# Two of the sixteen attention features of each head copied by DMA into the zero rows of the last block of gated features, for the output projection

## The chip, the cores and the metric

The kernel runs on one core of a Trainium2 chip. Its time is in device microseconds (us), the median of several executions. The core has a matrix engine (TensorE, PE in the profile; its weight loads are PEld), a vector engine (VectorE, DVE), an activation engine (ScalarE, ACT), a general engine (GpSimd, POOL) and a queue engine (SyncE, SP) from which this kernel issues every transfer. Transfers themselves run on sixteen DMA engines.

## What is computed

A normalised sequence x of 2048 tokens with 512 features goes through two branches, and both results are added to x. Branch A is attention with 32 heads of 16 features, where a token looks at 8 positions (itself and every second one before it), followed by a projection with `wo`. Branch B is a gated network: 688 features `z1`, gated by 688 others mixed over all tokens, and projected with `w_out`.

```python
xn = _layernorm(x, axis=-1)
return x + _A_ref(xn, A_wqkv, A_wo) + _B_ref(xn, B_w_in, B_w_sp, B_b_sp, B_w_out)
# _A_ref: S = 2048, D = 512, H = 32, Dh = 16, W = 8, dil = 2
o = jnp.einsum('bhsw,bhswd->bhsd', attn, vg)
return o.transpose(0, 2, 1, 3).reshape(B, S, D) @ wo
# _B_ref: Fh = 688
z = _gelu(jnp.einsum('bsd,df->bsf', x, w_in))
z1 = z[..., :Fh].copy()
z2 = _layernorm(z[..., Fh:], axis=-1)
g = jnp.einsum('ts,bsf->btf', w_sp, z2) + b_sp[None, :, None]
return jnp.einsum('bsf,fd->bsd', z1 * g, w_out)
```

## The kernel before

Tokens stand in 16 tiles of 128. The first part of the kernel (to about 75 us) normalises x, computes the second half of branch B's features, and queries, keys and values. The middle part runs from 75 to 172 us, one iteration a token tile `j`: `mix(j)` (L458) multiplies the tile's rows of `w_sp` with all of `z2`, `z1_tile(j)` (L470) computes the tile's `z1`, and `gate_out(j)` (L482) multiplies the two on DVE (L484) and issues from SP a transposing DMA (L485) that writes the gated tile into `uT`. `uT` holds features on partitions and tokens along its free axis, in 6 blocks (`MCH`) of 128 features. Only 688 of these 768 are real: the last block has 48 rows of features (`FTAIL`) and 80 rows of zeros, which come from columns of `z1` that POOL sets to zero (L478). The weights `wout` have the same 6 blocks; POOL sets the whole last block to zero (L511), and DMAs then fill the real rows (L562, L563).

Meanwhile DVE works through `av_ops` (L513): weighting of values by the attention, a tree of adds, and at L530 a write of `op`. `op` holds the attention output with one group of 256 tokens on each 32 partitions (one partition a head), the 16 features of a head (`DH`) and the two halves of the sequence (`hb`, 256 columns each) along its free axis. So partition 32k + h, feature d, column 256 hb + t is head h at token 1024 hb + 256 k + t. `vector_work(us)` (L538) lets DVE take the next pieces of that work between other instructions of its queue. The weights `wo_r` are laid out alike, a copy for each group of 32 partitions, by four DMAs (L566).

The last part, from 172 us, is the output projection (L574 to L598). It runs as two pairs; a pair is one half of the sequence. For each pair PE first runs, for both of its column blocks `jj`, for each `d` of 16 and each `k` of 4, a product of 32 rows (L583); the four `k` use four row groups of PE (`tile_position`) and four accumulators. Then for each of the 8 accumulators it adds the 6 blocks of `uT` times `wout` (L591), 128 rows each. When an accumulator is complete, DVE adds x to it (L595) and SP stores it (L596). The accumulators of a column block are one PSUM pool of four banks, so the second pair's products for a block start when the first pair's additions of that block are done. After each column block of the first pair, SP also loads the x rows for the second pair (`load_xr`, L548 and L550). The stores use four buffers `ot`.

The schedule is written by hand: each engine takes its instructions in the order of the text. SP issues transfers in that order, and before it issues one it waits for the transfer eight places earlier in its order, because eight completion semaphores are used in rotation.

Of the kernel before, what the change touches and what calls it, by code (L numbers as in the profile page):

```python
# [7 lines left out]
BF16 = mybir.dt.bfloat16  # L8
# [5 lines left out]
P = 128  # L14
S = 2048
D = 512
NT = S // P
C = D // P
H = 32
DH = 16  # L20
W = 8
DIL = 2
HALO = 16
NB = 2
SB = S // NB
NG = 4
TG = SB // NG
# [3 lines left out]
MCH = 6  # L31
# [13 lines left out]
def kernel(  # L45
# [18 lines left out]
    G = nc.gpsimd  # L64
    PE = nc.tensor
    SP = nc.sync
# [39 lines left out]
    for c in range(C):  # L106
# [3 lines left out]
                        base=15 - 128 * c, pattern=[[16, 32]], channel_multiplier=-1)  # L110
    mask = const.tile([32, W, HALO], F32, name="mask")
    G.memset(mask[:], 0.0)
    G.affine_select(out=mask[:], in_=mask[:], compare_op=ALU.is_ge, fill=NEG,
                    base=-DIL * (W - 1), pattern=[[DIL, W], [1, HALO]], channel_multiplier=0)
    b_col = const.tile([P, NT], F32, name="b_col")
# [14 lines left out]
    z2 = base.tile([P, NT, FH], BF16, name="z2")  # L130
    a_sb = base.tile([P, W, NB * TG], BF16, name="a_sb")
    vp = base.tile([P, DH, NB, HALO + TG], BF16, name="vp")
    w_z1 = base.tile([P, C, FH], BF16, name="w_z1")
# [127 lines left out]

    wv_v = wv[:].rearrange("p k (h d) -> p k d h", d=DH)
    xnT_g = xnT[:].rearrange("p c (b k t) -> p c b k t", b=NB, k=NG)
# [12 lines left out]
    def shifted(ap):  # L276

        return bass.AP(ap.tensor, ap.offset, [ap.ap[0], [DIL, 2]] + list(ap.ap[1:]))

    lg = [lgp.tile([P, W, TG], BF16, name="lg") for _ in range(NB)]  # L280
    prs = {}

    def products(hb, p):
        pr = prp.tile([P, 2, C, SB], BF16, name="pr")
        off = HALO - DIL * (W - 1 - 2 * p)
        V.tensor_tensor(pr[:], qk[hb][:, 0, :, HALO:HALO + SB].unsqueeze(1).broadcast_to([P, 2, C, SB]),  # L286
# [3 lines left out]
    def reduce_heads(hb, p):  # L290
        pr = prs.pop((hb, p))
        pl = ps_aux.tile([P, 2, TG], F32, name="pl", tag="aux")
        for c in range(C):
            for k in range(NG):
                PE.matmul(pl[32 * k:32 * k + 32, :, :], rsel[:, c, :], pr[:, :, c, k * TG:(k + 1) * TG],  # L295
                          start=(c == 0), stop=(c == C - 1), tile_position=(0, 32 * k))
        A.activation(lg[hb][:, 2 * p:2 * p + 2, :], pl[:], ACT.Copy, scale=float(DH) ** -0.5)

    def softmax_top(hb):
# [6 lines left out]
        V.tensor_tensor(m4[:, 0, :], m4[:, 0, :], m4[:, 1, :], ALU.max)  # L306
        V.tensor_tensor(l[:], l[:], m4[:, 0, :].unsqueeze(1).broadcast_to([P, W, TG]), ALU.subtract)

# [146 lines left out]
    uT = late.tile([P, MCH, S], BF16, name="uT")  # L455
    gate = {}

    def mix(j):  # L458
        pg = bank_pair("pg", j > 3)
        for k in range(NT):  # L460
            for hh in range(2):
                PE.matmul(pg[:, hh, 0:FHALF], wsps[j][:, k, :], z2[:, k, hh * FHALF:(hh + 1) * FHALF],  # L462
                          start=(k == 0), stop=(k == NT - 1))
        gs = gsp.tile([P, 2, FHALF], BF16, name="gs")
        A.activation(gs[:], pg[:, :, 0:FHALF], ACT.Identity, bias=b_col[:, j:j + 1])  # L465
        if j + 5 < NT:
            load_wsp(j + 5)
        return gs

    def z1_tile(j, gs):  # L470
        pz = bank_pair("pz1", j > 3)
        for hh in range(2):
            for kc in range(C):
                PE.matmul(pz[:, hh, 0:FHALF], xnT[:, kc, j * P:(j + 1) * P],  # L474
                          w_z1[:, kc, hh * FHALF:(hh + 1) * FHALF],
                          start=(kc == 0), stop=(kc == C - 1))
        z1 = z1p.tile([P, FPAD], BF16, name="z1")
        G.memset(z1[:, FH:FPAD], 0.0)  # L478
        A.activation(z1[:, 0:FH].rearrange("p (a b) -> p a b", a=2), pz[:, :, 0:FHALF], ACT.Gelu_apprx_tanh)  # L479
        gate[j] = (gs, z1)  # L480

    def gate_out(j):  # L482
        gs, z1 = gate.pop(j)
        V.tensor_tensor(z1[:, 0:FH], gs[:].rearrange("p a b -> p (a b)"), z1[:, 0:FH], ALU.mult)  # L484
        SP.dma_start_transpose(uT[:, :, j * P:(j + 1) * P], z1[:])  # L485
# [17 lines left out]
    late2 = ctx.enter_context(tc.tile_pool(name="late2", bufs=1, reuse_waits="tile", **right))  # L503
# [2 lines left out]
    smp = ctx.enter_context(tc.tile_pool(name="smp", bufs=1, reuse_waits="tile", **right))  # L506
    otp = ctx.enter_context(tc.tile_pool(name="otp", bufs=4, reuse_waits="tile", **right))
    op = late2.tile([P, DH, NB * TG], BF16, name="op")
    wo_r = late2.tile([P, DH, D], BF16, name="wo_r")
    wout = late2.tile([P, MCH, D], BF16, name="wout")  # L510
    G.memset(wout[:, MCH - 1, :], 0.0)  # L511

    def av_ops():  # L513
        for hb in range(NB):
            for q in range(2):
                osl = slice(hb * TG + q * P, hb * TG + (q + 1) * P)
                pws = []
                for p in range(4):
                    off = HALO - DIL * (W - 1 - 2 * p) + q * P
                    pw = pwp.tile([P, 2, DH, P], BF16, name="pw")  # L520
                    V.tensor_tensor(pw[:], shifted(vp[:, :, hb, off:off + P]),  # L521
# [16 lines left out]
    def vector_work(us):  # L538
        while us > 0:
            t = next(work, None)  # L540
            if t is None:
                return
            us -= t
# [4 lines left out]
    def load_xr(jj):  # L548
        xr = xrp.tile([P, NG, D], BF16, name="xr")
        SP.dma_start(xr[:], x_g[jj // 2, jj % 2])  # L550
        xrs.append(xr)

    vector_work(2.0)
    for j in range(3, NT):
        z1_tile(j, mix(j))
        if j == 3:
            pair_b.close()
            ps_o = [ctx.enter_context(tc.tile_pool(name="ps_o0", bufs=4, space=PSUM, reuse_waits="tile"))]
        vector_work(4.6)
        gate_out(j - 1)  # L560
        if j == 5:
            SP.dma_start(wout[:, 0:MCH - 1, :], B_w_out[0:(MCH - 1) * P, :].rearrange("(m p) n -> p m n", p=P))  # L562
            SP.dma_start(wout[0:FTAIL, MCH - 1, :], B_w_out[(MCH - 1) * P:FH, :])  # L563
        if 6 <= j < 10:
            k = j - 6
            SP.dma_start(wo_r[32 * k:32 * k + 32, :, :], A_wo.rearrange("(h d) n -> h d n", d=DH))  # L566
        if 11 <= j < 13:
            load_xr(j - 11)
    gate_out(NT - 1)
    pair_a.close()  # L570

# [2 lines left out]
    for pair in range(2):  # L574
        if pair:
            vector_work(1e9)
        pos = {}
        for jj in (2 * pair, 2 * pair + 1):
            for k in range(NG):
                pos[jj, k] = ps_o[jj % 2].tile([P, D], F32, name="po")  # L580
            for d in range(DH):
                for k in range(NG):
                    PE.matmul(pos[jj, k][:], op[32 * k:32 * k + 32, d, jj * P:(jj + 1) * P],  # L583
                              wo_r[32 * k:32 * k + 32, d, :],
                              start=(d == 0), stop=False, tile_position=(32 * k, 0))
        for jj in (2 * pair, 2 * pair + 1):
            hb, q = jj // 2, jj % 2
            for k in range(NG):
                i = 8 * hb + 2 * k + q
                for m in range(MCH):  # L590
                    PE.matmul(pos[jj, k][:], uT[:, m, i * P:(i + 1) * P], wout[:, m, :],  # L591
                              start=False, stop=(m == MCH - 1))
                vector_work(2.0)
                ot = otp.tile([P, D], BF16, name="ot")
                V.tensor_tensor(ot[:], pos[jj, k][:], xrs[jj][:, k, :], ALU.add)  # L595
                SP.dma_start(out2[i * P:(i + 1) * P, :], ot[:])  # L596
            if jj + 2 < 4:
                load_xr(jj + 2)  # L598
# [30 lines left out]
```

## Time and profile before

| What | us |
|---|---|
| median of 3 runs (212.54 to 212.78) | 212.76 |
| time of the profiled execution | 212.73 |
| its span in the profile | 210.8 |
| PE busy, of the span | 204.5 (97%) |
| DVE busy | 166.7 (79%) |
| ACT busy | 93.1 (44%) |
| 256 matmuls of 32 rows, L583 | 14.2 |
| 96 matmuls of 128 rows, L591 | 21.1 |
| 16 additions on DVE, L595 | 10.8 |

The span is the stretch that the profiler sees, from the first to the last event of the program; the time is longer by what lies around it. Busy times are sums over an engine's instructions. Matmuls overlap in PE's pipeline: the mean duration of one, 374 ns at L583, is its latency and not its share of PE's time, for which the busy time of the group or the chain of work is to be read. The granted clock of PE is full in every slice of the page.

### The profile page before, as it was taken

What the parts mean: (1) busy time and instruction counts of PE and PEld (TensorE: products, weight loads), DVE (VectorE), ACT (ScalarE), POOL (GpSimd) and SP (SyncE); (2) the same over time, 40 slices, a digit from 0 to 9 for tenths busy, and PEclk for the clock granted to TensorE, in tenths of its full rate; (3) what the DMA queues carried; (4) which work ended last, traced back from release to release, by engine and by line L of the source; (5) the groups of instructions that cost most, each with busy time, mean ns of one, the idle gap of its engine ahead of it and who ended that gap; (6) DMA issues with size and microseconds to landing.
All of it is one profiled execution on the core that took longest, in us unless ns stands there. A gap on an engine that the chain in (4) does not pass through costs nothing.

```text
span 210.8 us, 4012 instructions
## 1 busy us (share of the span) xinstructions
PE 204.5 (97%) x1677; PEld 119.2 (57%) x1677; DVE 166.7 (79%) x198; ACT 93.1 (44%) x144; POOL 6.0 (3%) x34
## 2 busy tenths in 40 slices
PE   7899999999999999999999999999999999999992
PEld 5445545445556665566666666666666654444440
DVE  4689977978169699999999999999999943771252
ACT  2457987766788997328522222222222220000000
POOL 5000000000000000000000000000000000000000
PEclk9999999999999999999999999999999999999999
DMA  6992444999000004533975899999763121048022
GB/s 174 316 331 65 83 82 96 153 278 194 3 0 3 3 0 37 124 63 76 170 172 113 218 212 176 199 192 183 157 167 92 37 40 37 25 115 262 28 100 75
DMA packets 67953, 25.56 MB, mean 121 GB/s; under 512 B 56880, under 2 KB 67808, under 8 KB 67808
## 3 DMA queue, kind: packets, MB, share of 16 engines
q1 hardware_dynamic: 67936, 25.31, 55.9%
q8 instruction: 13, 0.21, 0.4%
q14 instruction: 4, 0.03, 0.0%
HBM read 9.98 MB, written 2.10 MB: 57 GB/s over the span
## 4 chain that ended last, share of the span: by engine, by line
PE 94%; DMA 3%; DVE 1%; SPq 1%; ACT 0%; issue 0%
PE pg L462 36%; PE pq L257 13%; PE po L591 10%; PE pz L474 9%; PE pzb L225 9%; PE po L583 7%; PE pv L270 7%; PE pl L295 4%; DMA w_z<-in_B_w_in_dram 3%; DVE xnT L216 0%; DVE ot L595 0%; ACT xnT L214 0%; SPq L170 0%; PE pt L212 0%; SPq L166 0%
## 5 line engine op out<-in xcount | busy, mean ns | idle before, releaser
L462 PE MATMUL pg<-z,wspT 128*128 128x344 bf16 x512 | 77.3, 309 | 0.0
L462 PEld LDWEIGHTS <-wspT 128*128 128x128 bf16 x512 | 49.9, 98 | 25.2 <-issue 0.8
L286 DVE TENSOR_TENSOR pr<-qk 128x8192 bf16<-128x8192 bf16 x8 | 35.1, 4420 | 6.5 <-PE pl L295 6.5
L465 ACT ACTIVATE gs<-pg,b_col 128x688 bf16<-128x688 f32 x16 | 13.4, 835 | 54.0 <-PE pg L462 54.0
L521 DVE TENSOR_TENSOR pw<-vp,a_sb 128x4096 bf16<-128x4096 bf16 x16 | 36.1, 2284 | 0.0
L257 PE MATMUL pq<-xnT,wqk 128*128 128x512 bf16 x128 | 29.1, 379 | 0.4 <-DVE xnT L216 0.4
L595 DVE TENSOR_TENSOR ot<-po,xr 128x512 bf16<-128x512 f32 x16 | 10.8, 688 | 18.2 <-PE po L591 17.3
L225 PE MATMUL pzb<-w_z,xnT 128*128 128x344 bf16 x128 | 20.8, 310 | 0.9 <-DMA w_z<-in_B_w_in_dram 0.7
L474 PE MATMUL pz<-w_z,xnT 128*128 128x344 bf16 x128 | 21.3, 309 | 0.0
L591 PE MATMUL po<-wout,uT 128*128 128x512 bf16 x96 | 21.1, 379 | 0.0
L257 PEld LDWEIGHTS <-wqk 128*128 128x128 bf16 x128 | 12.3, 98 | 15.0 <-issue 1.4
L260 ACT CAST qk<-pq 128x1024 bf16<-128x1024 f32 x16 | 16.2, 1012 | 8.4 <-PE pq L257 8.2
L526 DVE TENSOR_TENSOR pw<-pw 128x4096 bf16<-128x4096 bf16 x8 | 18.3, 2288 | 0.1
L225 PEld LDWEIGHTS <-xnT 128*128 128x128 bf16 x128 | 12.1, 98 | 9.1 <-issue 1.7
L474 PEld LDWEIGHTS <-xnT 128*128 128x128 bf16 x128 | 12.4, 98 | 6.8 <-issue 0.8
L591 PEld LDWEIGHTS <-uT 128*128 128x128 bf16 x96 | 9.2, 98 | 11.7 <-issue 0.8
L270 PE MATMUL pv<-xnT,wv 128*32 128x512 bf16 x256 | 14.9, 380 | 0.0
L479 ACT ACTIVATE z<-pz 128x688 bf16<-128x688 f32 x16 | 11.9, 744 | 5.6 <-PE pz L474 4.8
L583 PE MATMUL po<-wo_r,op 32*128 32x512 bf16 x256 | 14.2, 374 | 0.0
L235 ACT ACTIVATE junk<-z 128x688 bf16<-128x688 bf16 x16 | 12.5, 780 | 0.1
L231 ACT ACTIVATE z<-pzb 128x688 bf16<-128x688 f32 x16 | 11.8, 739 | 0.6 <-PE pzb L225 0.6
L270 PEld LDWEIGHTS <-wv 128*32 128x32 bf16 x256 | 9.4, 138 | 4.7 <-issue 0.3
(73 smaller groups left out, 142.3 us busy)
## 6 DMA issues: line engine op xcount, KB each, us to landing
wo_r<-in_A_wo_dram SPq DMA_DIRECT2D x4, 512.0 KB, 5.4
xr<-in_A_x_dram SPq DMA_DIRECT2D x4, 512.0 KB, 4.1
out_dram<-ot SPq DMA_DIRECT2D x16, 128.0 KB, 1.7
xq<-in_A_x_dram SPq DMA_DIRECT2D x3, 512.0 KB, 6.7
wqk<-in_A_wqkv_dram SPq DMA_DIRECT2D x4, 256.0 KB, 6.2
w_z<-in_B_w_in_dram SPq DMA_DIRECT2D x2, 344.0 KB, 4.7
w_z<-in_B_w_in_dram SPq DMA_DIRECT2D x1, 688.0 KB, 6.9
wout<-in_B_w_out_dram SPq DMA_DIRECT2D x1, 640.0 KB, 5.4
```

Source lines behind the costliest of these rows:

```text
L225: PE.matmul(pz[:, hh, 0:FHALF], xnT[:, kc, i * P:(i + 1) * P], w_z2[:, kc, hh * FHALF:(hh + 1) * FHALF], start=(kc == 0), stop=(kc == C - 1))
L257: PE.matmul(pq[:, s, :], wqk[:, kc, s, c * P:(c + 1) * P], xnT[:, kc, tsl], start=(kc == 0), stop=(kc == C - 1))
L260: A.copy(qk[b // 2][:, :, c, at:at + 512], pq[:])
L270: PE.matmul(pv[32 * k:32 * k + 32, dd, :].rearrange("p (b t) -> p b t", b=NB), wv_v[:, kc, 2 * d2 + dd, :], xnT_g[:, kc, :, k, :], start=( ...
L286: V.tensor_tensor(pr[:], qk[hb][:, 0, :, HALO:HALO + SB].unsqueeze(1).broadcast_to([P, 2, C, SB]), shifted(qk[hb][:, 1, :, off:off + SB]), ...
L462: PE.matmul(pg[:, hh, 0:FHALF], wsps[j][:, k, :], z2[:, k, hh * FHALF:(hh + 1) * FHALF], start=(k == 0), stop=(k == NT - 1))
L465: A.activation(gs[:], pg[:, :, 0:FHALF], ACT.Identity, bias=b_col[:, j:j + 1])
L474: PE.matmul(pz[:, hh, 0:FHALF], xnT[:, kc, j * P:(j + 1) * P], w_z1[:, kc, hh * FHALF:(hh + 1) * FHALF], start=(kc == 0), stop=(kc == C - 1))
L521: V.tensor_tensor(pw[:], shifted(vp[:, :, hb, off:off + P]), a_sb[:, 2 * p:2 * p + 2, osl].unsqueeze(2).broadcast_to([P, 2, DH, P]), ALU.mult)
L526: V.tensor_tensor(pws[p - 1][:], pws[p - 1][:], pw[:], ALU.add)
L583: PE.matmul(pos[jj, k][:], op[32 * k:32 * k + 32, d, jj * P:(jj + 1) * P], wo_r[32 * k:32 * k + 32, d, :], start=(d == 0), stop=False, til ...
L591: PE.matmul(pos[jj, k][:], uT[:, m, i * P:(i + 1) * P], wout[:, m, :], start=False, stop=(m == MCH - 1))
```

## The change

PE's 32-row products now go over 14 of a head's 16 features (`DHA`). Features 14 and 15 are copied from `op` into rows 64 to 95 and 96 to 127 of the last block of `uT`, where zeros were: `op_rest(hb)` issues eight DMAs from SP for one half of the sequence, each with 32 partitions of 256 values (512 bytes a partition). The matching rows of `wo` are loaded into the same rows of the last block of `wout`, by two more DMAs. The copies for the first half are issued at the end of iteration 13 of the middle part, those for the second half between the two pairs of the output projection, when the last piece of `op` has been put in DVE's queue. POOL's zeroing of `wout` shrinks to rows 32 to 63, of which the load of the real rows then overwrites 32 to 47. The L591 matmuls are as many as before and have the same shape.

```diff
+DHA = 14
...
-    wo_r = late2.tile([P, DH, D], BF16, name="wo_r")
+    wo_r = late2.tile([P, DHA, D], BF16, name="wo_r")
     wout = late2.tile([P, MCH, D], BF16, name="wout")
-    G.memset(wout[:, MCH - 1, :], 0.0)
+    G.memset(wout[32:64, MCH - 1, :], 0.0)
+
+    def op_rest(hb):
+
+        for k in range(NG):
+            for e in range(2):
+                SP.dma_start(uT[64 + 32 * e:96 + 32 * e, MCH - 1, hb * SB + k * TG:hb * SB + (k + 1) * TG],
+                             op[32 * k:32 * k + 32, DHA + e, hb * TG:(hb + 1) * TG])
...
             SP.dma_start(wout[0:FTAIL, MCH - 1, :], B_w_out[(MCH - 1) * P:FH, :])
+            for e in range(2):
+                SP.dma_start(wout[64 + 32 * e:96 + 32 * e, MCH - 1, :],
+                             A_wo.rearrange("(h d) n -> d h n", d=DH)[DHA + e])
         if 6 <= j < 10:
             k = j - 6
-            SP.dma_start(wo_r[32 * k:32 * k + 32, :, :], A_wo.rearrange("(h d) n -> h d n", d=DH))
+            SP.dma_start(wo_r[32 * k:32 * k + 32, :, :], A_wo.rearrange("(h d) n -> h d n", d=DH)[:, 0:DHA, :])
         if 11 <= j < 13:
             load_xr(j - 11)
+        if j == 13:
+            op_rest(0)
...
         if pair:
             vector_work(1e9)
+            op_rest(1)
...
-            for d in range(DH):
+            for d in range(DHA):
                 for k in range(NG):
                     PE.matmul(pos[jj, k][:], op[32 * k:32 * k + 32, d, jj * P:(jj + 1) * P],
                               wo_r[32 * k:32 * k + 32, d, :],
```

## The prediction

> **What bounds the kernel now.** I read the chain of waits first, by engine, and then its last pieces in order of time (start, length, what). PE holds 94% of the chain, and the whole output projection is PE back to back, with one addition behind it.
>
> ```profile
> PE 94%; DMA 3%; DVE 1%; SPq 1%; ACT 0%; issue 0%
> ...
> 172.08 7.02 PE po L583 x128
> 179.10 10.47 PE po L591 x48
> 189.57 7.02 PE po L583 x128
> 196.59 10.48 PE po L591 x48
> 207.07 0.02 issue
> 207.09 0.69 DVE ot L595
> ```
>
> Nothing stands between these pieces: 172.08 + 7.02 = 179.10, and so on. So a matmul taken away here is time taken away, as long as nothing the projection reads comes late. What it reads in addition after the change comes from SP, so the second view is SP's timeline (start, time from the first issue to the end of the last, line):
>
> ```profile
> 160.31 14.73 SPq L485 DMA_TRANSPOSE uT<-z  x4
> 181.26 5.65 SPq L596 DMA_DIRECT2D out_dram<-ot  x4
> 186.96 0.43 SPq L550 DMA_DIRECT2D xr<-in_A_x_dram  x1
> 187.48 3.17 SPq L596 DMA_DIRECT2D out_dram<-ot  x4
> 190.71 0.43 SPq L550 DMA_DIRECT2D xr<-in_A_x_dram  x1
> 198.74 9.40 SPq L596 DMA_DIRECT2D out_dram<-ot  x8
> ```
>
> SP issues nothing from 191.14 to 198.74; the second half's copies fall there, right behind a load of 512 KB. The third view is the windows, which show how long that load occupies the DMA engines (the last two columns are their busy share and GB/s):
>
> ```profile
> 193.50:194.00 0.50, 0.50 (x16) 0.20 (x8) 0.00 (x0) 0.00 (x0) 0.00 (x0) 1.00 1.06 377
> 194.00:194.50 0.50, 0.50 (x16) 0.23 (x12) 0.00 (x0) 0.00 (x0) 0.00 (x0) 1.00 0.21 72
> 194.50:195.00 0.50, 0.50 (x16) 0.27 (x12) 0.00 (x0) 0.00 (x0) 0.00 (x0) 1.00 0.00 0
> ```
>
> They are idle by 194.5. The fourth is the list of DMA issues (line, count, KB each, median us from issue to landing):
>
> ```profile
> xr<-in_A_x_dram SPq DMA_DIRECT2D x4, 512.0 KB, 4.1
> out_dram<-ot SPq DMA_DIRECT2D x16, 128.0 KB, 1.7
> ...
> vp<-vp SPq DMA_DIRECT2D x1, 96.0 KB, 3.9
> wout<-in_B_w_out_dram SPq DMA_DIRECT2D x1, 48.0 KB, 5.4
> ...
> vp<-vp SPq DMA_DIRECT2D x1, 16.0 KB, 3.3
> ```
>
> **What is removed.** 2 features x 4 groups x 4 column blocks = 32 matmuls of L583. In the chain 128 of them take 7.02 us, 54.8 ns each, so 32 give 1.755 us, 0.88 in each pair. Bounds: the group's busy time, 14.2/256 = 55.5 ns, gives 1.78; the weight loads' pace, 6.59 us for a run of 128 (51.5 ns), gives 1.65. I take 1.755, the chain's own pace. L591 keeps its 96 matmuls and their shape; its zero rows were already multiplied, so filled rows cost PE nothing.
>
> **The new clock of the tail.** The first pair's L591 starts at 178.22 and ends at 188.69; the second pair's L583 ends at 188.69 + 6.14 = 194.83, L591 at 205.31. The addition and the last store follow as before: 210.8 - 1.755 = 209.05 span. The profiled execution took 212.73, so 210.98; it lies 0.03 below the median of 212.76, so the forecast for the median is 211.0.
>
> **The copies for the first half.** They follow the transposing DMA of tile 12, issued at 160.31 and lasting 1.21 (the median of L485), so from 161.5. Price of an issue: 0.33 (stores of 128 rows) to 0.58 (weight loads); the 48-row load of `wout` took 0.54, is nearest in shape, and with a gap of 0.06 gives 0.60. Eight: 4.8 us, to 166.3. Behind them SP has the transposes of tiles 13, 14 and 15. DVE finishes tile 13's gating at 165.20, so that transpose goes about 1.1 us later; tile 14's is gated at 170.03, not delayed. Tile 13 is read by the second pair's second column block, after 194.83: its landing (2.8 us after issue) has over 20 us of cover. The source is ready: the second L530 ended at 133.4. The eighth copy waits for tile 12's transpose, eight places before it, to land (163.1): already past. First reader: the sixth block of the first accumulator, 178.22 + 5 x 0.218 = 179.3 (10.48/48 = 0.218). Cover: 179.3 - 166.3 = 13.0 us, against landings of 1.7 to 5.4. Cost nothing; without that cover PE would stand for the landing itself.
>
> **The copies for the second half.** This is where the change can lose. The load of x in front of them comes after the first pair's last store, which follows PE, so 0.88 earlier: 189.83 to 190.26. The built order of instructions shows the eight copies right behind it and PE waiting for each group's two copies only at the sixth block of that group's first reader. At 0.60 each the issues start at 190.32, 190.92, ... 194.52. The first seven wait for stores and the x load before; the last of these, the store issued near 189.4, lands 1.7 to 4.3 us later (the median and the longest of L596), by 193.7, and the seventh copy's turn is 193.92. The eighth waits for the x load just issued, landing at 189.83 + 4.1 = 193.9 (4.5 at most: 194.3), before its turn at 194.52. Readers: weights for the sixth block are loaded one matmul ahead, so 194.83 + 4 x 0.218 = 195.7, and 1.31 later for each next group: 197.0, 198.3, 199.6. Second copies of the groups are issued at 190.92, 192.12, 193.32, 194.52. Landing: with 3.9 (the larger on-chip copy) they land at 194.8, 196.0, 197.2, 198.4, each 0.9 to 1.2 us in time. The two bounds: with 1.7 (a store) they are over 3 us in time, except the first group, which queues behind the x load to about 193.9 and still has 1.8. With 5.4 (a 48 KB load queued behind 640 KB) the first group lands at 196.3 and PE stands 0.6; the later ones are then in time. So the cost is 0 to 0.6; I take 0, by the on-chip rows and by engines that are idle from 194.5 - 0.88 = 193.6. The pair's first store, near 197.2, finds SP free since 195.1.
>
> The Trainium skill speaks against many small copies: the page DMA: Bandwidth & Descriptors, in its rules for kernel authors, says to coalesce many small transfers, since under 64 KB one pays mostly overhead; its section on the SWDGE path puts the fixed part of one at about 2.0 us. Each copy here has 16 KB. As an estimate from that page, eight paid one after another would be 16.3 us and end at 206.6, 7 us too late, some 218 us for the kernel; overlapped, they cost nothing. The trace shows overlap: the 640 KB and the 48 KB load of `wout` were issued 0.64 us apart (115.95 and 116.59) and each landed 5.4 us after its own issue.
>
> **The other edits.** Two more loads at the end of iteration 5 add 2 x 0.60 = 1.2 us to SP after 117.13, where it next issues at 118.45: they fit the gap, and that next load of `w_sp` is used five iterations later, near 29 us. `wo_r` shrinks by 64 KB a load; its last load is issued at 142.2 and read at 172. POOL's memset (0.52 us at 88.19, idle 52 us before it) gets no dearer. DVE: the first pair's additions follow PE and move with it; even if they kept their times, the last of the first block (186.3) comes before 188.69 and the last of the second (190.30) before 188.69 + 3.07 = 191.8. All of these: 0, bounded by those margins.
>
> **Rivals.** (1) The second half's copies land somewhat late, behind the x load. For: the engines are full to 194.5 in the trace, and margins are near 1 us. Against: on-chip rows. At 0.6 late it gives 211.6; its range is 211.2 to 212.3. (2) Each copy's issue costs what the second `vp` copy's did, 1.95 us, the only on-chip copy issued right behind another (the first, 0.77). Then the eighth starts at 190.32 + 7 x 2.0 = 204.3, lands at 207.6 against 199.6, and PE stands 8 us: 219. It costs more than the change gains once an issue takes over 1.1 us (190.32 + 7 x 1.1 + 3.3 = 201.3 = 199.6 + 1.75). Against: that copy had 512 pieces of 32 bytes behind 3072 others, these have 32 pieces of 512 bytes. (3) The saved matmuls don't shorten the path, because the second pair's products wait for freed accumulators, 212.8. For: the 0.42 us that weight loads stood before 189.50 is put down to an addition. Against: matmuls ran through that moment without a gap.
>
> **How the numbers follow.** Full gain, 211.0: 0.76, range 210.8 to 211.2. Rival 1: 0.12. Rival 2: 0.08. Rival 3: 0.04. The predicted time is 211.0; the range goes down to 210.7 for the removed matmuls' upper price and scatter, and up to 211.9, most of rival 1. A measurement of this kernel tells 0.2% (0.43 us, so 212.33) from no change. Faster: 0.76 and nearly all of rival 1, 0.87. Same: the rest of it and rival 3, 0.04. Slower: rival 2 and a little, 0.09.
>
> **What would show it.** L583 in the chain as 112 matmuls of about 6.14 us twice, L591 still 10.47 with no waits for `uT`; issues of the copies of 0.33 to 0.6 us; landings under 4 us. Wrong would be PE idle inside L591 of the second pair with a copy as its releaser, or issues over 1.1 us.

## The result, and the profile after

The changed kernel takes 211.09 us (median of 4 runs, 210.81 to 211.30), beside 212.65 us (4 runs) for the kernel before. The ratio is 0.9927, with a 95% interval of 0.9904 to 0.9951: 1.56 us faster. The forecast was 211.0, in a range of 210.7 to 211.9.

The end of the chain of waits after the change (start, length, what; lines of the kernel have moved, L583 is now L597, L591 is L605, L595 is L609, L596 is L610 and L550 is L558):

```profile
172.26 6.16 PE po L597 x112
178.42 0.16 issue
178.58 10.31 PE po L605 x47
188.88 6.15 PE po L597 x112
195.04 0.16 issue
195.20 10.32 PE po L605 x47
205.54 0.69 DVE ot L609
```

Each stretch of 32-row products has 112 matmuls in 6.15 us where there were 128 in 7.02, and the stretches of 128-row products are as long as before: 0.16 + 10.31 = 10.47. The 0.16 us of "issue" and the 47 in place of 48 are one missing record of a matmul each, not idle time: two later profiles of the same kernel show 48 matmuls in 10.47 us with nothing between.

The new transfers on SP:

```profile
160.49 1.21 SPq L486 DMA_TRANSPOSE uT<-z  x1
161.76 5.02 SPq L518 DMA_DIRECT2D uT<-op  x8
166.89 8.51 SPq L486 DMA_TRANSPOSE uT<-z  x3
...
186.09 0.42 SPq L558 DMA_DIRECT2D xr<-in_A_x_dram  x1
186.60 3.37 SPq L610 DMA_DIRECT2D out_dram<-ot  x4
190.03 0.87 SPq L558 DMA_DIRECT2D xr<-in_A_x_dram  x1
190.94 5.11 SPq L518 DMA_DIRECT2D uT<-op  x8
197.19 9.40 SPq L610 DMA_DIRECT2D out_dram<-ot  x8
```

The two blocks of eight copies (L518) lie where they were expected, and SP is free again at 196.05, before the first store of the second pair. In this profile the 16 copies of line L518 took 0.588 us of SP each (median) and 1.8 us from issue to landing (median, longest 4.6). The second copy of the second half, which completes group 0, has these two lines (issue: shortest, median, longest in ns; then landing):

```profile
L518 SPq DMA_DIRECT2D uT<-op x1: 589/589/589, 191.5 to 191.5; - x1
...
DMA to landing us min/median/max: 4.2/4.2/4.2
```

It lands at 191.5 + 4.2 = 195.7. Its reader, the weight load of the sixth block of the first accumulator, is due at 195.04 + 4 x 0.218 = 195.9. So the copy was about 0.2 us ahead of its reader. The gain is there, but little protected it in this execution.

### The profile page after: what moved, and what is told of

It is laid out like the page before. It is cut to its first block, busy times and chain, and to the rows that moved or that the text cites. A ratio compares the mean times of both kernels' runs of the same rounds, so it can differ in the third digit from the quotient of the medians.

```text
span 208.8 us, 3966 instructions
## 1 busy us (share of the span) xinstructions
PE 201.8 (97%) x1638; PEld 118.0 (57%) x1645; DVE 166.8 (80%) x198; ACT 93.1 (45%) x144; POOL 6.0 (3%) x34
## 4 chain that ended last, share of the span: by engine, by line
PE 94%; DMA 3%; DVE 1%; SPq 1%; issue 1%; ACT 0%
PE pg L463 36%; PE pq L258 13%; PE po L605 10%; PE pz L475 9%; PE pzb L226 9%; PE pv L271 7%; PE po L597 6%; PE pl L296 4%; DMA w_z<-in_B_w_in_dram 3%; DVE xnT L217 0%; DVE ot L609 0%; ACT xnT L215 0%; SPq L171 0%; PE pt L213 0%; SPq L167 0%
## 5 line engine op out<-in xcount | busy, mean ns | idle before, releaser
L609 DVE TENSOR_TENSOR ot<-po,xr 128x512 bf16<-128x512 f32 x16 | 10.9, 688 | 16.4 <-PE po L605 16.3
L605 PE MATMUL po<-wout,uT 128*128 128x512 bf16 x94 | 20.6, 379 | 0.3 <-issue 0.3
L605 PEld LDWEIGHTS <-uT 128*128 128x128 bf16 x96 | 9.2, 98 | 11.7 <-issue 0.8
L597 PE MATMUL po<-wo_r,op 32*128 32x512 bf16 x224 | 12.4, 374 | 0.0
L187 DVE BATCH_NORM_STATS2 stats<-xq 128x6 f32<-128x512 bf16 x16 | 10.7, 670 | 1.7 <-DMA xq<-in_A_x_dram 1.7
```

## The experiments

Every kernel was run beside the kernel before, in five rounds, on one chip for each group of runs; the kernel before had medians of 212.72, 213.09 and 212.66 us in the three groups. "Tail" is from the start of the first 32-row product in the timeline of PE to the start of the last addition. (Counted in the chain of waits, as the expectations do, it is 0.07 us shorter: 33.28 for 33.35.)

| Kernel | median us (range) | ratio to before, 95% interval | tail us |
|---|---|---|---|
| before (the profile shown above) | | | 35.08 |
| changed, first profile | 211.09 (210.81 to 211.30) | 0.9927 [0.9904, 0.9951] | 33.35 |
| changed, first group | 210.99 (210.55 to 211.93) | 0.9926 [0.9899, 0.9954] | 33.35 |
| one feature copied | 211.73 (211.23 to 212.90) | 0.9958 [0.9940, 0.9977] | 34.21 |
| copies only | 212.79 (212.07 to 213.24) | 0.9997 [0.9980, 1.0014] | 35.08 |
| no copies | 211.01 (210.69 to 211.14) | 0.9917 [0.9895, 0.9938] | 33.34 |
| group 0 last | 212.05 (211.53 to 213.16) | 0.9960 [0.9933, 0.9987] | 34.66 |
| copies earlier | 210.87 (210.25 to 213.35) | 0.9914 [0.9879, 0.9949] | 33.35 |
| copies between stores | 210.57 (210.27 to 211.21) | 0.9885 [0.9847, 0.9923] | 33.35 |
| changed, third group | 210.54 (210.20 to 211.33) | 0.9903 [0.9875, 0.9931] | 33.35 |
| copies between stores, third group | 210.78 (210.62 to 211.13) | 0.9911 [0.9885, 0.9937] | 33.35 |
| seventh block | 211.77 (210.80 to 213.67) | 0.9959 [0.9933, 0.9984] | 34.20 |

The tail is the sharper measure: scatter between executions arises before it, as the last section shows, and the tail itself repeats to 0.01 us.

**Is the gain the removed matmuls, and are the copies free?** Four kernels tell: the changed one again, one feature in place of two, the copies without the removal, and the removal without the copies.

The changed kernel again:

> The changed kernel once more, beside the others on the same chip, so that differences to it are read on one chip. Both theories: about 211.1 us, ratio to before near 0.9927. In its trace the first group's second copy for the second half is expected to land within 0.5 us of the weight load that needs it, with no idle time of PE inside the second pair.

It came out as expected in time and tail. The copy that completes group 0 was issued at 191.2 and landed 3.7 later, at 194.9; its reader was due at 194.79 + 0.87 = 195.66. The margin is 0.8 us here, not within 0.5.

One feature:

```diff
-DHA = 14
+DHA = 15
...
     G.memset(wout[32:64, MCH - 1, :], 0.0)
+    G.memset(wout[64:96, MCH - 1, :], 0.0)
...
-            for e in range(2):
-                SP.dma_start(uT[64 + 32 * e:96 + 32 * e, MCH - 1, hb * SB + k * TG:hb * SB + (k + 1) * TG],
-                             op[32 * k:32 * k + 32, DHA + e, hb * TG:(hb + 1) * TG])
+            SP.dma_start(uT[96:128, MCH - 1, hb * SB + k * TG:hb * SB + (k + 1) * TG],
+                         op[32 * k:32 * k + 32, DHA, hb * TG:(hb + 1) * TG])
...
-            for e in range(2):
-                SP.dma_start(wout[64 + 32 * e:96 + 32 * e, MCH - 1, :],
-                             A_wo.rearrange("(h d) n -> d h n", d=DH)[DHA + e])
+            SP.dma_start(wout[96:128, MCH - 1, :], A_wo.rearrange("(h d) n -> d h n", d=DH)[DHA])
```

> One feature (15) copied, 15 left for the 32-row products. If the gain is the removed matmuls at their own pace: 16 x 54.8 ns = 0.88 us off, ratio to before 0.9959, half of the full change. If the copies cost something of their own (a wait of PE, or contention), this version with half the copies saves more than half: the full change loses c, so this gives 0.88 - c/2 or less loss, and the two gains don't stand 1 to 2.

Its chain of waits:

```profile
171.52 6.59 PE po L595 x120
178.10 10.47 PE po L603 x48
188.57 6.59 PE po L595 x120
195.15 10.48 PE po L603 x48
```

7.02, 6.59 and 6.15 us for 128, 120 and 112 matmuls: the same step twice, 54.8 ns a matmul. The tails stand 0.87 and 1.73 us below the one before, 1 to 2, so no cost in proportion to the copies can be seen.

The copies alone (the edit is to the changed kernel):

```diff
-    wo_r = late2.tile([P, DHA, D], BF16, name="wo_r")
+    wo_r = late2.tile([P, DH, D], BF16, name="wo_r")
...
-    G.memset(wout[32:64, MCH - 1, :], 0.0)
+    G.memset(wout[:, MCH - 1, :], 0.0)
...
-            for e in range(2):
-                SP.dma_start(wout[64 + 32 * e:96 + 32 * e, MCH - 1, :],
-                             A_wo.rearrange("(h d) n -> d h n", d=DH)[DHA + e])
...
-            SP.dma_start(wo_r[32 * k:32 * k + 32, :, :], A_wo.rearrange("(h d) n -> h d n", d=DH)[:, 0:DHA, :])
+            SP.dma_start(wo_r[32 * k:32 * k + 32, :, :], A_wo.rearrange("(h d) n -> h d n", d=DH))
...
-            for d in range(DHA):
+            for d in range(DH):
```

> All sixteen copies stay, but PE runs its 32-row products over all 16 features and the last block's rows of wout stay zero, so the copied rows are multiplied by zero (the two extra weight loads are left out). If the copies are hidden: 212.7, ratio 1.000 within 0.001. If they cost something by themselves (DMA contention, PE waiting for them): slower than before, by 0.2 us or more.

The ratio is 0.9997 with 1 well inside the interval, and the tail is that of before, 35.08, to the last digit:

```profile
172.09 7.02 PE po L594 x128
179.11 10.47 PE po L602 x48
189.57 7.02 PE po L594 x128
196.59 10.48 PE po L602 x48
```

In this kernel the copies have more cover than in the changed one, because the second pair's 32-row products are 0.87 us longer and the first reader is due at 196.59 + 0.87 = 197.5. Whether the thin margin of the changed kernel costs anything is answered by the next kernel.

The removal alone (the edit is to the kernel before):

```diff
+DHA = 14
...
-    wo_r = late2.tile([P, DH, D], BF16, name="wo_r")
+    wo_r = late2.tile([P, DHA, D], BF16, name="wo_r")
...
-            SP.dma_start(wo_r[32 * k:32 * k + 32, :, :], A_wo.rearrange("(h d) n -> h d n", d=DH))
+            SP.dma_start(wo_r[32 * k:32 * k + 32, :, :], A_wo.rearrange("(h d) n -> h d n", d=DH)[:, 0:DHA, :])
...
-            for d in range(DH):
+            for d in range(DHA):
```

> 14 features in the 32-row products and no copies at all: features 14 and 15 of every head are left out of the output. If the copies are hidden: the same time as the changed kernel, 211.0, ratio to before 0.9918 to 0.993. If they give part of the gain back: faster than the changed kernel by that part, 0.2 us or more.

Its chain of waits:

```profile
171.80 6.16 PE po L584 x112
177.96 10.47 PE po L592 x48
188.42 6.15 PE po L584 x112
194.58 10.48 PE po L592 x48
```

Its tail is 33.34 against 33.35 with the copies, and its median is 0.02 us from that of the changed kernel on the same chip. So the copies are hidden, and the whole gain is that of the removed matmuls.

**How near is the cliff?** The order of the groups is turned round, so that the copies read first are issued last:

```diff
-        for k in range(NG):
+        for k in range(NG - 1, -1, -1):
             for e in range(2):
                 SP.dma_start(uT[64 + 32 * e:96 + 32 * e, MCH - 1, hb * SB + k * TG:hb * SB + (k + 1) * TG],
```

> The copies of each half are issued with group 3 first and group 0 last; nothing else. By the changed kernel's trace the last two copies of the second half are issued at 194.8 and 195.5 and land 1.8 later, at 197.3; the weight load of group 0's sixth block is due at 195.9. If the margin is as thin as that and only the late landing matters, PE stands 1.4 us there: about 212.5 us, ratio to before 0.999, 1.4 over the changed kernel. If PE's wait is hidden in some other way, or landings have more room than I read: 211.1, as the changed kernel.

The chain of waits now runs through the copies (start, length, what):

```profile
185.42 6.24 DMA xr<-in_A_x_dram
191.67 0.56 SPq L518
192.27 0.59 SPq L518
192.91 0.59 SPq L518
193.54 0.59 SPq L518
194.18 0.59 SPq L518
194.81 1.76 DMA uT<-op
196.70 9.46 PE po L605 x43
206.18 0.69 DVE ot L609
```

PE resumes at 196.70 when the last copy has landed; its timeline puts 1.16 us of idle time there, with the copy as its releaser:

```profile
194.52 1.03 PE L605 MATMUL po<-wout,uT 128*128 128x512 bf16 x4 [0.16 <-issue]
196.70 9.44 PE L605 MATMUL po<-wout,uT 128*128 128x512 bf16 x43 [1.16 <-DMA uT<-op]
```

The idle time counts from the end of the matmul before. The matmul at 196.70 would have had its turn at 194.52 + 4 x 0.218 = 195.39, so it is 1.31 us late, and that is the loss in the tail: 34.66, 1.31 us over the changed kernel, where 1.4 was expected. So three quarters of the gain in the tail are lost by the order of eight small transfers. By time it is a ratio of 0.9960, where 0.999 was expected, which lies just outside the interval. The first line shows something else: the third copy had to wait for the transfer eight places earlier, the x load issued at 185.42, which took 6.24 us to land. Here that held it by some 0.04 us only, because the second copy's issue had ended at 191.58. In the changed kernel's first profile the same wait held the third copy by 0.24 us: the second copy's issue ended at 192.10, the x load landed at 192.37 and the third copy went at 192.39.

**Does more room bring anything?** Two versions issue the second half's copies earlier. One puts them behind the first column block's stores and x load:

```diff
     for pair in range(2):
         if pair:
             vector_work(1e9)
-            op_rest(1)
...
             if jj + 2 < 4:
                 load_xr(jj + 2)
+            if jj == 0:
+                vector_work(1e9)
+                op_rest(1)
```

> The second half's copies are issued earlier, behind the first column block's four stores and the x load there, ahead of the second block's stores; the last pieces of op are queued on DVE by then anyway. If the copies are already hidden: the same as the changed kernel within 0.2 us (211.0), with the copies landing over 2 us before they are read. If the copies in the changed kernel take anything off the gain now and then: up to 0.2 us faster and a narrower spread. If stores moved back behind eight copies matter (four store buffers): slower, by up to 1 us.

The other puts a group's pair behind each store of the second column block:

```diff
-    def op_rest(hb):
+    def op_rest(hb, ks=range(NG)):
 
-        for k in range(NG):
+        for k in ks:
...
-            op_rest(1)
...
                 SP.dma_start(out2[i * P:(i + 1) * P, :], ot[:])
+                if jj == 1:
+                    op_rest(1, [k])
```

> The second half's copies are issued two at a time, each group's pair behind one store of the second column block, where SP waits for the next addition anyway. If hidden: 211.0, as the changed kernel, with copies that land over 1 us before they are read. It also prices an issue: if a back-to-back issue costs 0.59 and one after a pause 0.33 (as the stores), the first copy of a pair behind its store still costs near 0.5 to 0.6 and the store after it, which comes after a pause, 0.33.

Both have the tail of the changed kernel, 33.35. They took 210.87 and 210.57 us, 1.2 and 1.5 less than the kernel with group 0 last on the same chip. In the first one group 0's pair landed at 187.6 + 4.9 = 192.5, against a reader due at about 195.44 + 0.87 = 196.3. In the second one SP's timeline reads:

```profile
185.77 0.52 SPq L609 DMA_DIRECT2D out_dram<-ot  x1
186.33 1.16 SPq L518 DMA_DIRECT2D uT<-op  x2
187.59 0.53 SPq L609 DMA_DIRECT2D out_dram<-ot  x1
188.16 2.08 SPq L518 DMA_DIRECT2D uT<-op  x2
```

Stores cost 0.52 to 0.53 here and 0.33 in the last eight of the changed kernel. The guess that a store after a pair would cost 0.33 was made for one that comes after a pause; SP was behind, so none did (the store at 187.59 follows an issue that ended at 187.49). Right behind a pair, a store cost about what a copy does. The pair for group 0 landed at 186.9 + 4.8 = 191.7, against a reader due at about 194.20 + 0.87 = 195.1. Its median of 210.57 came from another chip, so it was set beside the changed kernel on one:

> The changed kernel beside the next two on one chip: about 211.0 us; the tail from the first 32-row product to the last addition 33.28 us, as in its two profiles so far.

> The version with the second half's copies between the stores, on one chip with the changed kernel. If the copies are hidden in both: the same tail of 33.28 us, and times that differ by no more than their scatter (0.2 us). If the thin margin of the changed kernel costs in some executions: this one faster by 0.2 to 0.4 us in the median, as the two earlier medians (210.57 against 210.99, on different chips) would have it.

210.54 for the changed kernel and 210.78 for this version, with tails equal to 0.01 us: more room brings no time in the runs made. No version here beats the changed kernel by more than the scatter.

**Where does the gain come from: rows that were zeros, or the 128-row form?** Four more features leave the 32-row products, and a 128-row block is added in their place, as a block filled with them would be:

```diff
-            for d in range(DHA):
+            for d in range(DHA - 4):
...
-                for m in range(MCH):
-                    PE.matmul(pos[jj, k][:], uT[:, m, i * P:(i + 1) * P], wout[:, m, :],
-                              start=False, stop=(m == MCH - 1))
+                for n, m in enumerate([0] + list(range(MCH))):
+                    PE.matmul(pos[jj, k][:], uT[:, m, i * P:(i + 1) * P], wout[:, m, :],
+                              start=False, stop=(n == MCH))
```

> On top of the change, four more features (10 to 13) are left out of the 32-row products, and each accumulator gets one more 128-row product instead (the first block of gated features a second time), as if those four features filled a block of their own; no further copies. The output lacks four features and has one block twice. If the gain of the change comes from rows that were multiplied as zeros anyway, and not from 128-row products being cheaper: 16 x 16 x ... per column block 16 x 54.8 = 877 ns off and 4 x 218 = 873 ns on, the same tail as the changed kernel, 33.28 within 0.1 us, 211.0. If 128-row products are the better form: faster, by 0.2 us or more a block.

The first pair answers the question, in the chain for the last stretch of the kernel:

```profile
172.00 4.43 PE po L597 x80
176.43 12.21 PE po L605 x56
...
191.77 3.24 DMA uT<-op
195.02 0.14 issue
195.15 10.97 PE po L605 x50
```

4.43 + 12.21 = 16.64 us, against 16.62 (6.15 + 10.47) in the changed kernel: the trade brings nothing. The expected tail was wrong all the same, 34.20 in place of 33.35. The second pair's 32-row products had been cover for the copies, and with 80 of them in place of 112 they are 1.72 us shorter (4.43 for 6.15), while the reader comes only one block, 0.22 us, later in its row. PE stands for a copy issued at 191.77:

```profile
192.99 1.47 PE L605 MATMUL po<-wout,uT 128*128 128x512 bf16 x6
195.15 10.95 PE L605 MATMUL po<-wout,uT 128*128 128x512 bf16 x50 [0.70 <-DMA uT<-op]
```

Against its turn at 192.99 + 6 x 0.218 = 194.30 the matmul is 0.85 us late, which is the whole difference of the tails.

## Why the prediction was right

**The bound.** The chain of before said that PE runs the projection without a gap, and that a matmul removed there is time removed. The four kernels on the gain show it: tails of 35.08, 34.21 and 33.35 for 128, 120 and 112 products a pair, with or without copies.

**The size.** 32 matmuls at 54.8 ns gave 1.755 us; the tail is 1.73 shorter. The other two prices in the prediction, 1.78 by the busy sum and 1.65 by the pace of weight loads, were both further off. Of the times, 212.65 - 211.09 = 1.56 in the first comparison and ratios from 0.9903 to 0.9927 in three lie round the forecast of 0.9917. The span did not give the size: it fell by 2.0 us, from 210.8 to 208.8, where the forecast had 209.05. But in the profiled executions the time outside the span rose from 1.9 us (212.73 - 210.8) to 2.4 (211.15 - 208.8), and from the start of the last addition to the end of the time it is 5.6 us in both (212.73 - 207.09 and 211.15 - 205.54).

**The first half's copies.** An issue of 0.60 with its gap and an end at 166.3 were expected; it was 0.63 (5.02/8) and 166.78. Landing was 1.8 us each, over ten before the first reader. The transpose behind them went at 166.89, about 1.5 us after its tile was ready (166.89 - 165.4), where a delay of 1.1 was forecast, and nobody waited for it.

**The second half's copies.** The outcome, no wait, was right. The margin was less well judged. I had the x load ahead of the copies land 4.1 us after its issue, 4.5 at most, with a margin of 0.9 for group 0. In the first profile the two x loads of this stretch landed 6.3 and 5.3 us after issue, the second took 0.87 to issue, and the copies started at 190.94 in place of 190.32: margin 0.2. In the two other profiles it was 0.8 and 0.9 (190.4 + 3.7 = 194.1 against 194.12 + 0.87). So in the first profile the forecast of no wait held by 0.2 us; with so little to spare it was in part luck. The copy's landing followed that of the x load: in the three profiles the load landed at 195.3, 194.5 and 193.7, and the copy that completes group 0 at 195.7, 194.9 and 194.1, 0.3 to 0.4 us behind it each time. The price taken for landing, 3.9 by the larger on-chip copy, was near for group 0 (3.7 to 4.2) and too high for the later groups (down to 1.8), so the safe side was group 3 and not, as the prediction had it, all groups nearly alike (0.9 to 1.2).

**The other edits** were put at nothing, and nothing shows. From the landing of the first load of weights, a piece of the chain that the last section shows, to the first 32-row product it is 172.01 - 7.71 = 164.30 us in the kernel before and 172.19 - 7.88 = 164.31 in the changed one. (One reading there is a little off: the last addition of the first block, put at 186.3, ended at 186.36.)

**Rival 1, late copies,** did not happen in the change, but its mechanism is real: with group 0 last PE stood, and with less cover too. **Rival 2, 1.95 us an issue,** did not happen: 0.59 is the rule. Single copies took more, 1.04 with the copies earlier, 1.45 and 1.56 between stores and 1.50 in the kernel with the copies only; but an x load took 1.44 in the kernel without copies, so it is not the copies alone. The prediction's range for an issue, 0.33 to 0.58, left out one of 1.37 that the trace of before has, a load of `wo_r` at 122.45. An issue's price is no constant, then, though no run made eight of them dear. What makes single ones dear, and why the second `vp` copy took 1.95, was not tried. **Rival 3, freed accumulators,** fell with the equal steps of the chain: the second pair's products shorten from 7.02 to 6.59 and 6.15 us like the first's.

The Trainium skill's advice against many small copies (DMA: Bandwidth & Descriptors, rules for kernel authors) concerns their overhead. The overhead is there: by the medians 0.59 us of SP and 1.8 us of landing for 16 KB. Hidden behind PE it cost nothing that could be measured, as the copies alone show with a ratio of 0.9997.

## What to carry to other kernels

The rows of zeros that padded the contraction here were free room on the matrix engine, which bounds this part of the kernel: work moved into them came off the bound, 54.8 ns for each small product. The room ends where the zeros end, because four 32-row products in four row groups cost here what one 128-row product does (4 x 54.8 = 219 ns against 218). When small transfers feed the bounding engine, issue them in the order in which they are read; the same copies in the wrong order took back 1.3 of 1.73 us. And look at what stands before them in the queue: here the pair that is read first landed 0.3 to 0.4 us behind a load of 512 KB, whenever that landed, and a load eight places earlier once held a copy for 0.24 us.

## What the runs showed that I had not expected

Executions differ by some tenths of a microsecond, and the profiles show one place where they do: the first load of weights. Its piece of the chain of waits in the changed kernel's three profiles and in the one with the copies earlier was 5.62, 5.38, 4.70 and 6.03 us; the first 32-row product then started at 172.19, 171.95, 171.27 and 172.60, in the same order and at the same distances. For the last two:

```profile
2.26 4.70 DMA w_z<-in_B_w_in_dram
```

```profile
2.26 6.03 DMA w_z<-in_B_w_in_dram
```

So 1.33 us between two executions of kernels with equal tails are settled before the first product of these weights, and one profiled execution's time should not be compared with another's where half a microsecond matters. This does not explain every long execution: the two longest of the kernel with the copies earlier, 212.84 and 213.35 us, ran at a mean granted clock of 0.990 and 0.991, the longest with the seventh block, 213.67, at 1.000, and none of these three was profiled.

And the landing time of a load belongs to its surroundings: the x loads of 512 KB took 4.0 to 4.5 us in the kernel before, and up to 6.3 us in the changed one, whose first one of this stretch was issued before any copy of the second half. In the kernel without copies the two of this stretch took 4.2 and 4.7, and with the seventh block, where the copies are there, 4.0 and 4.8, so the copies are not shown to be the cause. What made those two slower was not tried.
